# A new hand-written order for the passage from the long convolution into the gated MLP: half-sized copies and turns, another norm path for the first tiles, more filler matmuls

## The chip, the core and the metric

One core of a Trainium2 chip runs the whole program. It has five instruction queues: PE (TensorE: matmuls, with the weight loads shown apart as PEld), DVE (VectorE), ACT (ScalarE), POOL (GpSimd) and SP (SyncE, which issues most DMAs). Each queue runs its own instructions strictly in the order in which the program gave them; queues wait for each other through semaphores. The metric is the device time of one execution in microseconds, lower is better. Before the change it is 304.9 us (median of three runs, 304.87 to 305.95).

## The reference, cut to what matters

Sequence 2048 (16 tiles of 128), width 640 (five units of 128 columns), one batch, bf16.

```python
mod = (silu(c) @ w_mod).reshape(1, 6, 1, -1)            # sa, ca, ga, sb, cb, gb
h = layernorm(x) * (1 + ca) + sa
k_shift = short_conv(A_k, shift_k); kv = k_shift * A_v
y = irfft(rfft(kv, 2S) * rfft(ssm_k, 2S))[:S] + kv * ssm_D
x = x + ga * (h * y)                                     # first half: long convolution, gated
h = layernorm(x) * (1 + cb) + sb
z = gelu(h @ w_in); z1 = z[:, :864]; z2 = layernorm(z[:, 864:])
g = w_sp @ z2 + b_sp
out = x + gb * ((z1 * g) @ w_out)                        # second half: gated MLP mixed along the sequence
```

## The kernel before, in words

The program is a list of 1444 operations, each with a function, a kind and the engines that may run it. A string at the top, `ORDER`, lists all of them once: `P208` means "operation 208, on PE". `Plan.run` walks the string and issues each operation on the engine that its letter names. Nothing else sets the order: on each engine the instructions stand as the string has them, and the framework adds the semaphore waits. Since each operation is numbered by where it is made, inserting one renumbers all that follow.

The first half works unit by unit (u = 0 to 4). Below, `T4_2` is the tile of unit 4, step 2; each unit has eight steps (0 to 7) of two frequency blocks. The kinds that matter, with the lines under which the profile shows them:

- `fwd` (PE, L275, `pu<-X,M`): forward transform of a step into the PSUM tag `pu`, which has two buffers; `pk4_5` is the same for the filter of unit 4, step 5.
- `khc` (ACT, L278, `KH<-pu`): the filter's transform copied out, `KH4_5`.
- `prod` (DVE, L495, `Tf<-pu,KH` or `T<-pu,KH`): the product of a step's `pu` and `KH`. In steps 0, 2, 4, 5, 7 it is written in f32 and two `csum` (L509, `W<-Tf`, POOL or DVE) follow; steps 1, 3, 6 go straight to the inverse.
- `inv` (PE, L275, `pz<-W,G` or `pz<-T,G`): inverse transform into the PSUM tag `pz` (two buffers). `zc` (L278, `Z<-pz`, ACT or DVE): its copy into `Z`.
- `zt` (SP, L777): for units 0 to 3 a DMA turns `Z` into `ZT`; `y` (PE, `sm<-Ebd,ZT`) and `ym` (DVE, L770) make the last transform and multiply it into the gate `gh`.
- `ghm` (L753, POOL or DVE): the modulation of a gate piece, `gh(u, g)`: first times `gca`, then plus `gsa`. `res` (L808): adds a gate piece into the residual `xt`. `ln2` (DVE, L814): statistics of a piece of a row. `modc` (PE): the columns of one modulation vector.

Unit 4 is last, and its `Z` is turned by PE: `zfl` (L831) transposes, `zk` (L278, `X<-pu`, `X<-pz`) copies out, `yl` (PE, `<-Ebd,X`) makes the last transform for four tiles at a time, `yml` (DVE, L856) multiplies, `res` adds, `ln2` and `ag2` (L943) give mean and variance of each row.

The MLP then needs its first tiles. Group 0 (tiles 0 to 3) goes in two pieces of two tiles: `rstd2` (POOL, L218 adds the epsilon, L219 raises to -0.5), `nmr2` (DVE, L947), `zx` (L957 ACT, L959 POOL, L961 DVE: the normalised tile), `hfl` (PE, L972: transposes), `hmod` (L985 DVE, L983 ACT), and then `zz` (PE, L275, `pu<-big,Z` and `pz<-big,Z`: five matmuls of 128x432 each, 16 `zz` to a group of four tiles, four groups) with `gelu` (ACT, L1034). Groups 1 to 3 are turned by a DMA instead (`turn`, L1003, then `hmod2`, L1011). After the last `zz` comes the mixing along the sequence (L1126) and the output projection (L1335, L1348).

`fill` operations are matmuls on the identity, 128x512, whose result is never read (`s<-ident`). They share the PSUM tag `s1`, which has one buffer.

## Time and profile before

| | |
|---|---|
| time of three runs | 304.87, 304.90, 305.95 us |
| span of the profiled execution (first to last instruction) | 303.8 us |
| busy: PE, DVE, POOL, ACT | 293.1, 260.4, 186.8, 164.0 us |
| mean granted TensorE clock | 0.989 |

The profile gives the profiled execution's span alone; a timed run holds 1.1 us beside it (304.9 against 303.8).

A row of the timeline reads: start in us, duration in us, engine, line, operation, output and inputs by tile, shapes, how many instructions were merged (`x2`), and in square brackets how long the engine sat idle before it and which engine released it. Rows of the chain of work read: start, us, engine, tile, line. Rows of the stretches read: from:to, length, busy time of PE, PEld, DVE, ACT, POOL (with the number of instructions), the granted clock of TensorE (1.00 is full), the DMA share and GB/s. Rows of the groups read: line, engine, operation, tiles, shapes, count, busy us, mean ns of one, idle time before. The mapping of a row to an operation of the list is by tile, line and order.

### The profile page before, as it was taken

Reading aid. Unit: us, or ns where it says so; the run is one execution under the profiler, and the core shown is the slowest. Engines: PE = TensorE matmul, PEld = TensorE weight load, DVE = VectorE, ACT = ScalarE, POOL = GpSimd, SP = SyncE. Lnnn points to the kernel's source line nnn. Section 1 sums busy time; section 2 is a strip of 40 time slices with the busy share of each in tenths; the row PEclk is TensorE's granted clock in tenths of the full one; section 3 lists DMA queues with packets and bytes.
Section 4 is the critical chain, followed back from the end, with each engine's and each line's share of the span. In section 5 each row is a group of like instructions: output and inputs, shape, how many; then the busy total and the mean of one; then the engine's idle time right before and its main releaser. Section 6 shows DMA issues by size and latency. Waiting matters only on the chain.

```text
span 303.8 us, 7152 instructions
## 1 busy us (share of the span) xinstructions
PE 293.1 (96%) x2827; PEld 207.0 (68%) x2827; DVE 260.4 (86%) x527; ACT 164.0 (54%) x299; POOL 186.8 (61%) x213
## 2 busy tenths in 40 slices
PE   6899999999999999799999999999999999999996
PEld 2788999999989988645555555555555555665664
DVE  8899999999989999989595988988678798886794
ACT  5989999998888865446665779500111102111110
POOL 5463788839769997577537342099531863476771
PEclk9999999999999999869999999999999999999999
DMA  7999869792397978005997900057654446452433
GB/s 143 270 242 271 194 177 282 134 223 39 77 186 163 287 122 276 2 2 105 157 234 154 197 0 4 0 117 150 132 133 90 102 112 141 102 84 73 91 83 121
DMA packets 117155, 41.57 MB, mean 137 GB/s; under 512 B 102557, under 2 KB 117122, under 8 KB 117122
## 3 DMA queue, kind: packets, MB, share of 16 engines
q1 hardware_dynamic: 116968, 41.08, 62.0%
q8 instruction: 22, 0.36, 0.5%
q14 instruction: 11, 0.09, 0.1%
q10 hardware_dynamic: 154, 0.05, 0.1%
HBM read 16.60 MB, written 2.63 MB: 63 GB/s over the span
## 4 chain that ended last, share of the span: by engine, by line
PE 80%; DVE 8%; SPq 5%; DMA 3%; issue 2%; POOL 1%; ACT 0%; DVEq 0%; POOLq 0%
PE ps L1126 23%; PE pu L275 19%; PE pz L275 17%; PE po L1335 5%; PE sm L275 5%; PE s L275 4%; SPq L570 3%; DVE Tf L495 3%; PE po L1348 3%; DMA ZT<-in_A_v_dram 3%; PE pz L1126 2%; PE pu L1126 1%; DVE Z L616 1%; SPq L585 1%; DVE ot L1394 1%
## 5 line engine op out<-in xcount | busy, mean ns | idle before, releaser
L275 PEld LDWEIGHTS <-Z 128*128 128x128 bf16 x320 | 32.0, 100 | 28.8 <-issue 3.0
L275 PE MATMUL pu<-X,M 128*128 128x128 bf16 (+1 forms) x480 | 45.6, 237 | 0.9 <-DVE Tf L495 0.7
L509 POOL TENSOR_TENSOR W<-Tf 128x256 bf16<-128x256 f32 x42 | 30.7, 745 | 15.0 <-DVE Tf L495 9.0
L275 PEld LDWEIGHTS <-M 128*128 128x128 bf16 x480 | 36.7, 98 | 4.2 <-issue 1.6
L1126 PEld LDWEIGHTS <-S 128*128 128x128 bf16 x256 | 25.0, 98 | 20.8
L275 PE MATMUL pu<-big,Z 128*128 128x432 bf16 x160 | 34.6, 360 | 0.0
L278 ACT CAST X<-s 128x1024 bf16<-128x1024 f32 x32 | 32.7, 1021 | 3.3 <-PE s L275 3.2
L275 PE MATMUL pz<-big,Z 128*128 128x432 bf16 x160 | 33.0, 349 | 0.0
L495 DVE TENSOR_TENSOR Tf<-pu,KH 128x1024 f32<-128x1024 f32 x25 | 30.3, 1215 | 1.2 <-ACT Z L278 0.5
L1132 ACT COPY m<-ps 128x432 f32<-128x432 f32 x7 | 3.6, 521 | 49.8 <-PE ps L1126 41.0
L1126 PEld LDWEIGHTS <-wT 128*128 128x128 bf16 x192 | 18.8, 98 | 15.3
L278 ACT CAST Z<-pz 128x512 bf16<-128x512 f32 x40 | 23.5, 596 | 4.9 <-PE pz L275 4.7
L275 PEld LDWEIGHTS <-G 128*128 128x128 bf16 x330 | 24.6, 98 | 1.8 <-issue 0.4
L278 ACT CAST KH<-pu 128x512 bf16<-128x512 f32 x40 | 23.1, 592 | 3.8 <-PE pu L275 3.4
L1126 PE MATMUL ps<-X,wT 128*128 128x432 bf16 x112 | 22.7, 346 | 0.0
L1126 PE MATMUL ps<-X,S 128*128 128x432 bf16 x112 | 22.6, 346 | 0.0
L1040 DVE BATCH_NORM_STATS2 stz<-X 128x6 f32<-128x432 bf16 x32 | 18.1, 588 | 5.0 <-ACT X L1034 4.9
L1126 PE MATMUL ps<-T,S 128*128 128x432 bf16 x112 | 22.2, 346 | 0.0
L275 PE MATMUL sm<-dg,big 128*128 128x128 bf16 x320 | 20.7, 219 | 1.1 <-DVE Z L616 1.0
L275 PEld LDWEIGHTS <-big 128*128 128x128 bf16 x320 | 18.9, 98 | 2.0 <-issue 1.6
L495 DVE TENSOR_TENSOR T<-pu,KH 128x1024 bf16<-128x1024 f32 x15 | 18.2, 1215 | 1.9 <-PE pu L275 1.8
L275 PEld LDWEIGHTS <-X 128*128 128x128 bf16 x288 | 17.8, 98 | 2.2 <-POOL X L433 0.7
(223 smaller groups left out, 666.7 us busy)
## 6 DMA issues: line engine op xcount, KB each, us to landing
wm<-in_w_mod_dram SPq DMA_DIRECT2D x6, 800.0 KB, 4.9
xt<-in_A_q_dram SPq DMA_DIRECT2D x4, 640.0 KB, 5.6
out_dram<-ot SPq DMA_DIRECT2D x15, 160.0 KB, 1.9
big<-in_B_w_in_dram SPq DMA_DIRECT2D x2, 1080.0 KB, 7.8
X<-in_A_ssm_k_dram SPq DMA_DIRECT2D x4, 512.0 KB, 6.2
ZT<-in_A_v_dram SPq DMA_DIRECT2D x1, 1024.0 KB, 7.6
big<-in_A_v_dram SPq DMA_DIRECT2D x1, 1024.0 KB, 7.8
w_o<-in_B_w_out_dram SPq DMA_DIRECT2D x6, 160.0 KB, 3.5
```

Of the source, the lines that this page charges most:

```text
L275: nc.tensor.matmul(o, lhsT=w, rhs=x, start=start, stop=stop)
L278: (e.copy if e is nc.scalar else e.tensor_copy)(dst, src)
L495: e.tensor_tensor(T_[:], (tl[pu] if src is None else tl[src])[:, :, :, None, :].to_broadcast(shape), tl[KH][:, :, None, :, :].to_broadcast ...
L509: e.tensor_tensor(tl[W][:, :, o, :], T_[:, :, 0, o, :], T_[:, :, 1, 1 - o, :], op=ALU.add if o else ALU.subtract)
L570: e.dma_start_transpose(k_of(u)[:, KPAD + h * m:KPAD + (h + 1) * m], A_k[0, h * m:(h + 1) * m, u * DU:(u + 1) * DU])
L585: e.dma_start(v_of(0, ns.start, NT // n) if u0 == 0 else tl[name][:], v_nat[:, ns, ds])
L616: e.tensor_tensor(dst, tl[ps][:].rearrange("p n (c g) -> p n c g", g=8), v_of(u, i * SCH, SCH).rearrange("p n (c g) -> p n c g", g=8), op= ...
L1040: op("D", "stz", lambda e, i=i, n=n, fc=fc: e.bn_stats(out=stz[:, n, fc, :], in_=tl[z2][:, i, fc * FC:(fc + 1) * FC]), r=[(z2, (i, fc))], ...
L1126: nc.tensor.matmul(ps[:, :FC], lhsT=lhs[:, s_, :], rhs=rhs(s_), start=(s_ == 0 and not more), stop=(s_ == HT - 1), skip_group_check=more)
L1132: e.copy(part[p, m][:], part[p, BANK[m]][:, :FC])
L1335: nc.tensor.matmul(ps[:, :HS], lhsT=w(k), rhs=x(k), start=start and k == 0, stop=stop and k == n - 1, skip_group_check=True)
L1348: e.matmul(po[t, i][:, :hi - lo], lhsT=uTs[t][:fsz[ft], ft, :], rhs=T["w_o"][:fsz[ft], ft, lo:hi], start=(ft == 0), stop=(ft == NFT - 1))
```

## The change

The program has 1462 operations afterwards. `ORDER` is new; up to its 486th entry it runs the same operations on the same engines in the same order, and so do its last 359. What is added or split:

- step 4 of unit 4 (`LAST = 4`, which is the last inverse in either list): its `zc` in two halves of 128x256.
- unit 4's `zfl`: each of four batches of eight transposes in two halves, and each `zk` in two halves of 128x512. In the new list DVE copies both halves of batch 16, the first of batch 8 and the second of batch 24; ACT the other four.
- `yl` of the first four tiles in eight parts instead of four.
- first piece of group 0 (`quick`): the epsilon is added by DVE in the second `ag2`, POOL only raises to -0.5, `nmr2` is gone, and both `zx` run on DVE (before: ACT and POOL).
- `hfl`: by tile instead of by half of the columns.
- unit 4's `res` of groups 1 to 3 may run on POOL (the new list leaves them on DVE).
- six more `fill` of one matmul each; the passage holds `fill8`, `fill7`, `fill4` and the old `fill1` of two matmuls; `fill6` and `fill5` stand far earlier, `fill9` behind the last `zz`.

The two lists decoded, engine by engine, from the product `T3_7` to the passage (number pairs in brackets are unit and group of a gate piece):

```
POOL before: csum W3_5b, ghm(3,3), csum W3_7 x2, ghm(3,0), ghm(4,2), csum W4_0 x2, W4_2 x2, ghm(3,0), csum W4_5 x2,
             W4_7 x2, W4_4a, res(2), ghm(4,1), ghm(4,3), rstd2
POOL after:  csum W3_5b, ghm(3,3), ghm(3,0), ghm(3,0), ghm(4,2), csum W3_7 x2, W4_0 x2, W4_2 x2, W4_5 x2, res(2),
             csum W4_7 x2, W4_4a, res(2), ghm(4,1), res(3), res(3), rstd2
DVE before:  prod T3_7, ym, sbc, ln2 x3, ym, T4_0, ym, T4_3, T4_2, ym, T4_5, T4_1, T4_7, T4_6, T4_4, csum W4_4b, ym, ym,
             ln2, ym, zk, ym, zk, ...
DVE after:   prod T3_7, ghm(4,3), ym, sbc, ln2 x3, ym, ym, ym, zc Z3_7, T4_0, T4_2, T4_5, T4_3, T4_1, T4_7, T4_6, T4_4,
             csum W4_4b, ln2, ym x4, zk x4 (halves), ...
PE before:   inv 3_6, y, fwd pu4_3, inv 3_7, y, pu4_2, modc, pk4_5, pu4_5, pu4_1, inv 4_0, 4_3, pu4_7, inv 4_2, pu4_6,
             inv 4_1, pu4_4, inv 4_5, 4_7, y, 4_6, y, 4_4, y, zfl ...
PE after:    inv 3_6, pu4_2, y, y, modc, inv 3_7, pu4_5, inv 4_0, pk4_5, pu4_3, pu4_1, pu4_7, inv 4_3, 4_2, pu4_6,
             inv 4_1, pu4_4, fill8, inv 4_5, 4_6, y, y, 4_7, 4_4, y, y, zfl halves ...
ACT before:  zc Z3_5, Z3_6, Z3_7, khc KH4_5, gelu table, cbc, zc Z4_0, ...
ACT after:   gelu table, zc Z3_5, Z3_6, cbc, khc KH4_5, zc Z4_0, ...
SP before:   zt ZT3, load w_mod 5, load w_in 0;  after: zt ZT3, load w_in 0, load w_mod 5
```

PE in the passage, after: zfl halves, yl x8, fill7, fill4, yl of tiles 4-7 and 12-15, modc, fill1, vturn, hfl, hfl, yl of tiles 8-11, zz. Before: zfl, modc, yl x4, vturn, yl x3, hfl, hfl, fill1, zz.

The diff, without the string and with its main hunks:

```diff
+LAST = 4
-FILLS = (4, 2, 2, 2, )
+FILLS = (4, 2, 2, 2, 1, 1, 1, 1, 1, 1)
...
-            op("AD", "zc", lambda e: copy(e, tl[Z][:, :, 2 * KP * st:2 * KP * (st + 1), :], tl[pz][:]
+            parts = KP if u == NU - 1 and st == LAST else 1
+            for h in range(parts):
+                k0, k1 = h * KP // parts, (h + 1) * KP // parts
+                op("AD", "zc", lambda e, k0=k0, k1=k1: copy(e, tl[Z][:, :, 2 * (KP * st + k0):2 * (KP * st + k1), :], tl[pz][:, k0:k1]
...
-                tag, k = "pz" if g % 2 else "sm", 4 if g == 0 else 1
+                tag, k = "pz" if g % 2 else "sm", 8 if g == 0 else 1
...
         def norm_piece(g, p, ns, xn2):
+            quick, gs = g == 0 and p == 0, slice(ns[0], ns[-1] + 1)
             for n in ns:
-                op("D", "ag2", lambda e, n=n: e.bn_aggr(out=mv2[:, n, :], in_=st2[:, n, :, :]),
+                def aggregate(e, n=n):
+                    e.bn_aggr(out=mv2[:, n, :], in_=st2[:, n, :, :])
+                    if quick and n == ns[-1]:
+                        e.tensor_scalar(mv2[:, gs, 1], mv2[:, gs, 1], EPS, None, op0=ALU.add)
...
-                op("DAG", "zx", norm, r=[("mv2", n), ("rs2", (g, p)), ("nm2", (g, p))] + [("xt", (u, n)) for u in range(NU)] + ([] if first else [(xn2, "new")]),
+                op("D" if quick else "DAG", "zx", norm, r=[("mv2", n), ("rs2", (g, p))] + ([] if quick else [("nm2", (g, p))]) + [("xt", (u, n)) for u in range(NU)] + ([] if first else [(xn2, "new")]),
```

## The prediction

> **What bounds the kernel now.** I read the page first, then the chain of work in order of time, then stretches for the granted clock, then the timeline of the passage and of the ten microseconds ahead of it.

> ```profile
> span 303.8 us, 7152 instructions
> PE 293.1 (96%) x2827; PEld 207.0 (68%) x2827; DVE 260.4 (86%) x527; ACT 164.0 (54%) x299; POOL 186.8 (61%) x213
> PEclk9999999999999999869999999999999999999999
> ```

> ```profile
> 118.44 0.59 ACT Z L278
> ...
> 129.72 3.60 PE pu L275 x10
> 133.32 2.14 PE pz L275 x10
> ...
> 139.67 1.82 PE pu L275 x10
> ```

> ```profile
> 120.18:123.59 3.41, 3.41 (x112) 3.32 (x109) 3.24 (x9) 2.35 (x4) 0.91 (x1) 1.00 0.22 75
> 123.59:127.00 3.41, 1.98 (x76) 1.88 (x73) 2.96 (x14) 0.92 (x1) 2.13 (x4) 1.00 0.02 5
> 127.00:130.42 3.42, 2.64 (x15) 1.38 (x13) 3.42 (x11) 1.02 (x2) 2.48 (x4) 0.50 0.00 0
> 130.42:133.83 3.41, 3.41 (x11) 1.37 (x9) 3.41 (x13) 1.35 (x2) 3.29 (x4) 0.50 0.00 0
> 134.00:191.00 57.00, 57.00 (x322) 30.82 (x320) 46.13 (x133) 39.83 (x75) 28.02 (x31) 1.00 0.58 114
> ```

> PE bounds the whole; from 134 to 191 it is never idle (57.00 of 57). So a gain in the passage reaches the end only as an earlier, or faster, start of the `zz` stream. The stream starts at 129.72 at half clock (10 matmuls in 3.60 us, later in 1.82) and is at full clock from 133.83. Its first 20 matmuls end at 133.32 + 2.14 = 135.46; at full clock they take 3.64, so the stream stands as if it had begun at 131.8. That is the mark to beat. The half clock costs (133.83 - 129.72)/2 = 2.05 us.

> **Passage, part by part.** From the first transposes (119.08) to the stream:

> ```profile
> 119.08 1.07 PE L831 MATMUL pu<-ident,Z 128*128 128x128 bf16 x16 [0.44 <-ACT Z L278]
> 121.31 1.01 ACT L278 COPY X<-pz 128x1024 bf16<-128x1024 bf16 x1
> 124.43 0.19 POOL L218 TENSOR_SCALAR rstd<-mv 128x2 f32<-128x2 f32 x1 [3.34 <-DVE mv L943]
> 124.70 0.81 POOL L219 TENSOR_TENSOR rstd<-rstd,mhalf 128x2 f32<-128x2 f32 x1
> 125.75 0.92 ACT L957 ACTIVATE Z<-xt,nmr,rstd 128x640 bf16<-128x640 bf16 x1 [2.57 <-DVE nmr L947]
> 125.88 0.87 POOL L959 TENSOR_SCALAR Z<-xt,rstd,nmr 128x640 bf16<-128x640 bf16 x1 [0.36 <-DVE nmr L947]
> 126.81 0.67 PE L972 MATMUL s<-ident,Z 128*128 128x128 bf16 x6 [1.43 <-POOL Z L959]
> 127.58 1.05 DVE L985 TENSOR_SCALAR Z<-s,cb_col,sb_col 128x256 bf16<-128x256 bf16 x3
> 128.00 1.02 ACT L983 ACTIVATE Z<-sm,sb_col,cb_col 128x256 bf16<-128x256 bf16 x2 [1.33 <-PE sm L972]
> 128.69 1.03 PE L275 MATMUL s<-ident 128*128 128x512 bf16 x2 [0.78 <-DVE Z L985]
> L961 DVE TENSOR_SCALAR Z<-xt,mv,rstd 128x640 bf16<-128x640 bf16 x6 | 2.7, 482 | 0.0
> L278 ACT CAST Z<-pz 128x512 bf16<-128x512 f32 x40 | 23.5, 596 | 4.9 <-PE pz L275 4.7
> ```

> - `zc` in halves, both on ACT behind each other: 128x512 takes 0.60 and 128x1024 1.01, so 256 columns take about 0.4, two of them 0.8: a cost of 0.2.
> - `zfl`/`zk` in halves: the last copy ends at 121.31 + 1.01 = 122.32, that is 3.24 after the first transpose. Eight half batches at PE's 0.9 per 16 transposes end at 1.8, seen by ACT at 2.0; ACT's four halves start at about 0.66 and take between 0.5 (half of 1.01) and 0.6 each, the last ending at 2.65. Gain 0.6.
> - Epsilon on DVE: POOL's add costs 124.70 - 124.43 = 0.27, the DVE instruction about 0.1. Gain 0.15.
> - No `nmr2`, both `zx` on DVE: before, pow ends at 125.51 and the later `zx` at 126.75, 1.24 later; two at 0.48 take about 0.9. Gain 0.35. DVE's `ln2`, `yml`, `res` queued behind `ag2` (about 1.0) lie beside POOL's pow.
> - `hfl` by tile: five transposes stand behind the last tile, not ten at half clock: 0.77 (126.81 to 127.58) becomes about 0.5. Gain 0.3.
> - The two-matmul filler moves ahead of `hfl`: before, `hmod` ends at 129.02 and the stream starts at 129.72. Gain 0.7.

> Sum: 2.1 less 0.2, say 2.0 with bounds 1.5 and 2.4. If the clock holds through the passage, 2.05 more. `fill9` stands behind the last `zz` with PE busy: one 128x512 matmul, half of the old pair at full clock, costs 0.2. `fill5` and `fill6` cost the same, up to 0.5 with a wait for their PSUM buffer, but they lie ahead of a point where POOL is late (next part); if that cover goes they cost 0.4 to 1.0. So the passage is worth 2.0 + 2.05 - 0.2 = 3.85.

> **The ten microseconds ahead of it: a new wait.** The new list also rearranges what feeds the last inverse.

> ```profile
> 103.75 1.15 POOL L753 TENSOR_TENSOR gh<-gh,gsa_bf 128x512 bf16<-128x512 bf16 x1
> 104.86 1.41 POOL L509 TENSOR_TENSOR W<-Tf 128x256 bf16<-128x256 f32 x2
> 106.24 2.26 POOL L753 TENSOR_TENSOR gh<-gh,gca_bf 128x512 bf16<-128x512 bf16 x2
> 105.94 1.23 DVE L495 TENSOR_TENSOR Tf<-pu,KH 128x1024 f32<-128x1024 f32 x1
> 107.24 0.60 PE L275 MATMUL pz<-W,G 128*128 128x256 bf16 x6
> 108.98 0.60 PE L275 MATMUL pu<-X,M 128*128 128x256 bf16 x6
> 109.62 0.58 ACT L278 CAST KH<-pu 128x512 bf16<-128x512 f32 x1 [1.16 <-PE pu L275]
> 114.28 1.21 DVE L495 TENSOR_TENSOR T<-pu,KH 128x1024 bf16<-128x1024 f32 x1
> 115.42 1.21 DVE L495 TENSOR_TENSOR Tf<-pu,KH 128x1024 f32<-128x1024 f32 x1
> 116.77 0.98 POOL L509 TENSOR_TENSOR W<-Tf 128x256 bf16<-128x256 f32 x1 [0.85 <-DVE Tf L495]
> 117.80 0.60 PE L275 MATMUL pz<-W,G 128*128 128x256 bf16 x6
> L278 DVE CAST X<-pu 128x512 bf16<-128x512 f32 x3 | 2.0, 681 | 0.0
> ```

> Before, the two sums of `W3_7` run on POOL at 104.86, right behind `ghm(3,3)` (103.75), and three gate multiplies come later. In the new list the three stand ahead of the sums. POOL has no idle time there, so the sums start at 104.86 + 3 x 1.13 = 108.25 and end at 109.6. Step by step:

> 1. `inv 3_7` at 109.65 (before 107.24). Its copy `zc Z3_7` is now on DVE, in front of all products of unit 4: it can start 0.64 later (as `khc` follows `fwd`, 108.98 to 109.62), 110.3, and at 0.68 with overlap lets `T4_0` start at 110.9. Before: 105.94. DVE, which had four `ym` and a `ghm` to do, is idle from about 108.5.
> 2. `T4_0` ends at 112.1, its two sums on POOL at 113.6, `inv 4_0` at 113.65. In PE's queue `pk4_5` is now behind that inverse: 114.1, its copy on ACT from 114.75 to 115.33, and `T4_5` needs it: 115.4. DVE was done with `T4_2` at 113.2: 2.2 us idle.
> 3. Five more products at a pitch of 1.14 (114.28 to 115.42) put `T4_4` at 121.1; the two `pu` buffers and inverses ahead of the `fwd` in PE's queue add 0.5 (next free buffer) to 1.35 (buffers in turn: `pu4_3` waits for `T4_5`). So `T4_4` starts at 121.6 to 122.45 where it started at 115.42: 6.2 to 7.0 late, and its POOL sum, the last inverse (117.80) and the first transposes with it.

> PE meanwhile has little to do. The clock fell at 127.00 and rose at 133.83, 6.83 or 2 x 3.41 apart, so I cut stretches of 3.41 from there and count streamed columns, at 1.82 us for ten times 432 (0.42 ns each).

> ```profile
> 122.82 1.76 PE L275 MATMUL pz<-Ebd,X 128*128 128x16 bf16 x64
> 124.43 0.95 PE L275 MATMUL sm<-Ebd,X 128*128 128x16 bf16 x32
> ```

> The stretch 123.59 to 127.00 holds some 65 of these transforms and four transposes, 1550 columns, 0.65 us: half clock followed. 120.18 to 123.59 holds 16 transposes (2048 columns, 0.86 us) and some 60 transforms, about 1.3 us with the rest: it did not. In the new kernel 109.94 to 113.35 has the end of `inv 3_7` and `pu4_5` (1024 columns), about 0.6 us. By this the clock falls at 113.35, and returns only after a full stretch: 127.00 to 130.42, with PE 2.64 of 3.42 busy, did not bring it back, 130.42 to 133.83 did. From 113.35 each `fwd` takes 0.86 and each direct inverse (2048 columns) 1.72. `T4_5` comes at 116.3. With buffers in turn PE has gaps until 119.8, so full clock returns at 123.59 and `T4_4` ends at 126.6 (116.63 before): 10.0 late. With the next free buffer PE is nearly full from 116.76 on, the clock may return at 120.18, and `T4_4` is 7.7 late. Ends 7.7 and 10.0; no row decides between them, and I take 8.4, a little under the middle, because the low end needs fewer waits.

> [...]

> **Sum.** Delay 8.4 less 3.85: 4.55 slower, against the span 303.8 gives 308.35; with the 1.1 us that a timed run holds beside the span, 309.4 (median of three runs 304.9, to which the same is added). Without the clock's fall it is 6.2 to 7.0 less 3.85: 307.3 to 308.1. With it, 7.7 to 10.0 less 3.85: 308.8 to 311.1.

> Left at nothing: POOL's two `res(3)` ahead of `rstd2` (four operations of 1.15 behind the last sum end about 3.1 after the first transposes, `rstd2` is due at 4.7); `zt` of unit 3 leaves 2.5 us later but its reader `y` does too, and more; `w_in` 0 and `w_mod` 5 change places on SP, both due after 130. The first tiles of group 1:

> ```profile
> 138.88 3.00 SPq L1003 DMA_TRANSPOSE Z<-Z  x1
> 143.97 1.65 POOL L1011 TENSOR_SCALAR Z<-Z,cb_col,sb_col 128x512 bf16<-128x512 bf16 x2 [1.41 <-ACT X L1034]
> ```

> They are ready at about 145.6 and wanted at 131.8 + 16 x 0.91 + 0.6 = 147: 1.4 of slack. In the new list the DMA leaves about 7.7 after the stream starts, lands 5.1 later and needs 2 more: 14.8 against 15.2. I take no stall; at worst 1 us.

> **The rivals.**
> - *The stall without the half clock* (time 307.3 to 308.1, middle 307.7): for it, the stretch's 0.6 us of columns are hardly under the 0.65 that lost the clock, and another cut of the stretches would hold more; against it, PE is idle there for longer than in the stretch that lost it.
> - *The other side: the products run back to back on DVE.* Place: DVE from 103.5 to 117. If POOL's sums and `KH4_5` come before DVE asks for them, the delay is only the work put in front: `ghm(4,3)` at 0.5 and `zc` at 0.6, 1.1, less 3.85: 302.15. It decides below a delay of 2.35 (over 0.5% faster). For it: before, DVE's products stand 1.14 apart there without a wait. Against: POOL's 3 x 1.13 stand in one queue ahead of the sums, without idle time.
> - *Half of it:* `W3_7` comes in time but `KH4_5` does not: `T4_0` at 109.1, `T4_4` 4.3 to 5.1 late, 305.35 to 306.15: no change that can be told.
> - *The passage loses the clock too.* The stretch over the fillers, `hfl` and `yl` has about 1.4 us of columns (four fillers 0.86, ten transposes 0.54), hardly more than the one that kept it. If it falls, up to 2.05 more than the forecast: 311.45. [...]

> **How the numbers follow.** Stall with half clock 0.45, and with the passage's fall as well 0.1; stall alone 0.2; half of it 0.12; back to back 0.13. A measurement of this kernel tells about 0.5% (1.5 us) from no change: 303.4 to 306.4. Faster 0.13, same 0.12, slower 0.75. The range leaves out the back-to-back case and a little at the top: 305.0 to 311.3; the likeliest case's own is 308.8 to 311.1.

> **What would show it.** Right: DVE idle ahead of `zc Z3_7` and again ahead of `T4_5`; POOL with three gate multiplies in a row ahead of the sums of `W3_7`; a granted clock of 0.5 somewhere between 113 and 124; the last inverse 7 to 10 us later than 117.80; and from the first transposes to the stream 8.5 to 9 us instead of 10.64, at clock 1.00. Wrong: `T4_0` starting before 108, or the last inverse within 2 us of its old place; or the passage at half clock as before.

## The result, and the profile after

| | before | after |
|---|---|---|
| time, median of five runs | 305.21 us (304.87 to 305.95) | 314.1 us (313.5 to 315.46) |
| ratio | 1 | 1.0292, 95% interval 1.0265 to 1.0320 |
| span of the profiled execution | 303.8 us | 313.7 us |

The change makes the kernel 8.9 us slower, about twice the 4.5 us of the forecast. The profiled execution of the changed kernel is the slowest of its five runs (315.46), so its span shows a little more than the medians do: 9.9. A timed run holds 1.7 to 1.9 us beside its span wherever both are on record (315.46 against 313.7), not 1.1; the span of 303.8 belongs to a time of about 305.6. The difference that was forecast is not touched by this. A few executions of 389 to 610 us, in some of the experiments, are left out of every median and ratio below.

The mean granted clocks of the five executions are 0.973 (the profiled one), 0.984, 0.984, 0.984 and 0.978. A mean of 0.973 over 313.7 us is 16.9 us at half clock, five stretches of 3.41; a mean of 0.984 is some 10 us, three stretches. So what is said below of where the clock was lost holds for the profiled execution. Where the other four lost it, no trace shows.

The page of the changed kernel, the lines that answer to those of before:

```profile
span 313.7 us, 7168 instructions
PE 299.5 (95%) x2833; PEld 211.3 (67%) x2833; DVE 266.2 (85%) x530; ACT 163.1 (52%) x299; POOL 190.5 (61%) x214
PEclk9999999999999976959999999999999999999999
```

There are now three slices with a lowered clock instead of two, and PE is busy 6.4 us longer (299.5 against 293.1) with six matmuls more: it works more slowly, and hardly more.

To see where the time went I put the two timelines beside each other at products on DVE. Before, the last one ahead of the first difference of the lists and `T3_7`:

```profile
76.36 1.21 DVE L495 TENSOR_TENSOR T<-pu,KH 128x1024 bf16<-128x1024 f32 x1
102.40 1.22 DVE L495 TENSOR_TENSOR Tf<-pu,KH 128x1024 f32<-128x1024 f32 x1
```

After, the same two, then DVE, PE and POOL up to the last product, `T4_4`:

```profile
77.13 1.21 DVE L501 TENSOR_TENSOR T<-pu,KH 128x1024 bf16<-128x1024 f32 x1
104.22 1.20 DVE L501 TENSOR_TENSOR Tf<-pu,KH 128x1024 f32<-128x1024 f32 x1
...
109.47 1.29 DVE L779 TENSOR_TENSOR gh<-gh,sm 128x512 bf16<-128x512 bf16 x2 [1.28 <-PE sm L281]
111.48 0.69 DVE L284 CAST Z<-pz 128x512 bf16<-128x512 f32 x1 [0.72 <-PE pz L281]
112.08 2.35 DVE L501 TENSOR_TENSOR Tf<-pu,KH 128x1024 f32<-128x1024 f32 x2
117.48 1.23 DVE L501 TENSOR_TENSOR Tf<-pu,KH 128x1024 f32<-128x1024 f32 x1 [3.05 <-ACT KH L284]
125.26 1.23 DVE L501 TENSOR_TENSOR Tf<-pu,KH 128x1024 f32<-128x1024 f32 x1 [0.16 <-PE pu L281]
...
110.21 0.76 PE L281 MATMUL sm<-sc_bf,wm 128*128 128x1 bf16 x25 [0.54 <-DVE gh L779]
110.84 0.60 PE L281 MATMUL pz<-W,G 128*128 128x256 bf16 x6
113.35 1.01 PE L281 MATMUL pu<-X,M 128*128 128x256 bf16 x6 [1.91 <-DVE Tf L501]
...
109.25 1.41 POOL L515 TENSOR_TENSOR W<-Tf 128x256 bf16<-128x256 f32 x2
```

And the passage with the first of the stream, and the two waits at the stream's end:

```profile
129.00 1.07 PE L842 MATMUL pu<-ident,Z 128*128 128x128 bf16 x16
131.77 0.61 PE L842 MATMUL pz<-ident,Z 128*128 128x128 bf16 x8 [1.26 <-ACT X L284]
133.35 0.42 DVE L870 TENSOR_TENSOR gh<-gh,sm 128x256 bf16<-128x256 bf16 x1
135.99 0.80 DVE L979 TENSOR_SCALAR Z<-xt,mv,rstd 128x640 bf16<-128x640 bf16 x2
136.40 1.01 PE L281 MATMUL s<-ident 128*128 128x512 bf16 x2
137.54 0.50 PE L993 MATMUL s<-ident,Z 128*128 128x128 bf16 x3
139.49 2.36 PE L281 MATMUL pu<-big,Z 128*128 128x432 bf16 x10
203.02 1.63 PE L1148 MATMUL pz<-X,S 128*128 128x432 bf16 x8 [0.91 <-DVE S L1123]
209.23 1.62 PE L1148 MATMUL pz<-T,wT 128*128 128x432 bf16 x8 [0.19 <-DVE c L1177]
```

Read together (times of before from its rows above and in the prediction, and from this one for its first `zz`):

```profile
129.51 3.81 PE L275 MATMUL pu<-big,Z 128*128 128x432 bf16 x10
```

| point | before | after | later by |
|---|---|---|---|
| last product ahead of the first difference | 76.36 | 77.13 | 0.77 |
| `T3_7` | 102.40 | 104.22 | 1.82 |
| `T4_0` | 105.94 | 112.08 | 6.14 |
| `T4_4` | 115.42 | 125.26 | 9.84 |
| first `zfl` | 119.08 | 129.00 | 9.92 |
| first `zz` | 129.51 | 139.49 | 9.98 |
| end of the span | 303.8 | 313.7 | 9.9 |

0.77 belongs to the two executions (the lists are the same up to there). The rest is lost between 77 and 125 us, and the passage wins nothing back. The stretches of 3.41 us, cut at the changes of the clock (113.0, 123.2, 133.4 and 140.3), show the clock halved twice, in the stall and again in the passage:

```profile
109.55:112.97 3.42, 1.35 (x36) 1.11 (x32) 2.70 (x4) 1.16 (x4) 1.12 (x2) 1.00 0.02 5
112.97:116.38 3.41, 2.49 (x17) 1.94 (x17) 1.46 (x2) 0.00 (x0) 2.77 (x4) 0.50 0.96 184
...
130.03:133.45 3.42, 2.16 (x50) 1.77 (x48) 2.13 (x7) 2.15 (x4) 2.13 (x2) 1.00 0.00 0
133.45:136.86 3.41, 3.35 (x93) 2.62 (x91) 3.27 (x13) 0.17 (x1) 0.71 (x1) 0.50 0.02 5
```

### The profile page after: what moved, and what is told of

It reads as the page before. It is cut to its first block, busy times and chain, and to the rows that moved or that the text cites. A ratio compares the mean times of both kernels' runs of the same rounds, so it can differ in the third digit from the quotient of the medians.

```text
span 313.7 us, 7168 instructions
## 1 busy us (share of the span) xinstructions
PE 299.5 (95%) x2833; PEld 211.3 (67%) x2833; DVE 266.2 (85%) x530; ACT 163.1 (52%) x299; POOL 190.5 (61%) x214
## 4 chain that ended last, share of the span: by engine, by line
PE 31%; DVE 12%; SPq 4%; DMA 3%; POOL 2%; issue 1%; DVEq 0%
PE ps L1148 22%; PE po L1357 5%; PE po L1370 2%; DVE st L823 2%; SPq L1110 2%; DMA Z<-Z 2%; DVE stz L1062 1%; DMA wT<-in_B_w_sp_dram 1%; DVE T L1133 1%; SPq L1220 1%; DVE xt L817 1%; SPq L1025 1%; POOL S L1123 1%; DVE Z L1033 1%; POOL rstd L225 1%
## 5 line engine op out<-in xcount | busy, mean ns | idle before, releaser
L281 PE MATMUL pu<-X,M 128*128 128x128 bf16 (+1 forms) x480 | 48.1, 243 | 3.4 <-DVE Tf L501 2.2
L281 PEld LDWEIGHTS <-Z 128*128 128x128 bf16 x320 | 31.3, 98 | 27.0 <-DVE Z L1007 0.2
L281 PEld LDWEIGHTS <-M 128*128 128x128 bf16 x480 | 38.3, 100 | 8.3 <-issue 5.1
L281 PE MATMUL pu<-big,Z 128*128 128x432 bf16 x160 | 32.8, 349 | 0.0
L281 PEld LDWEIGHTS <-G 128*128 128x128 bf16 x330 | 25.9, 101 | 2.9 <-issue 0.9
L284 ACT CAST Z<-pz 128x512 bf16<-128x512 f32 (+1 forms) x40 | 22.8, 586 | 8.3 <-PE pz L281 7.9
L281 PE MATMUL sm<-dg,big 128*128 128x128 bf16 x320 | 21.9, 226 | 0.1
L281 PEld LDWEIGHTS <-big 128*128 128x128 bf16 x320 | 20.1, 102 | 0.9 <-issue 0.4
```

What stands on the lines that cost most here:

```text
L281: nc.tensor.matmul(o, lhsT=w, rhs=x, start=start, stop=stop)
L284: (e.copy if e is nc.scalar else e.tensor_copy)(dst, src)
```

## The experiments

The theory to begin with: nearly the whole loss arises ahead of the last inverse, through three new waits (POOL's sums of `W3_7`, the copy of `Z3_7` on DVE, the matmuls of `KH4_5`) and the half clock that they bring. The rival: the stretch costs 4 to 5 us and the halves of the passage the rest. "Ratio" is to the kernel before, measured beside it.

**1. The stretch put back.**

```diff
 ORDER of the changed kernel, from the first difference to zc Z4_4:
-  the new order
+  the order of before on all engines (fill5, fill6, fill8 stay behind the same PE operations)
 POOL behind csum W4_4:
-  res(3), res(3), rstd2
+  ghm(4,1), ghm(4,3), res(3), rstd2, res(3), res(2)
```

> The changed kernel, but with the order of before on all engines from the first difference up to the last inverse (the added fillers of that stretch stay), and on POOL up to the first rstd2. Passage and stream as changed. Theory A (the waits ahead of the last inverse are nearly the whole loss): the last inverse stood 9.65 us late, 1.8 of it was there before the stretch, so about 8 less than 314.1: 306.1 with the clock falling in the passage as in the changed kernel, 304 if it holds there. Theory B (the stretch is worth what was forecast for it less the passage's gain, 4 to 5, and the halves cost the rest): 309.5 to 310.

308.5 us, ratio 1.0084 (1.0057 to 1.0111). So 1.0292 - 1.0084, 2.1% or 6.3 us, lies in the stretch: between the two theories (8, and 4 to 5). The trace says more: the first `zfl` stands 119.79 - 103.23 = 16.56 behind `T3_7`, where it stood 16.68 behind it before and 24.78 in the changed kernel, so the whole stall (8.1) is gone. 2.6 us of loss are left. One place of it was my own: POOL's two additions now ran beside the two `zx`, which took 1.24 each where they take 0.40 in the changed kernel (135.99, two in 0.80):

```profile
126.65 2.41 POOL L815 TENSOR_TENSOR xt<-xt,gh 128x512 bf16<-128x512 bf16 x2
126.77 2.47 DVE L977 TENSOR_SCALAR Z<-xt,mv,rstd 128x640 bf16<-128x640 bf16 x2
```

**2. One wait at a time.** Three kernels, each the changed one with one move:

```diff
 e2, POOL:  -ghm(3,0), ghm(3,0), ghm(4,2), csum W3_7, csum W3_7
            +csum W3_7, csum W3_7, ghm(3,0), ghm(3,0), ghm(4,2)
 e3, PE:    -pu4_5, inv 4_0, pk4_5
            +pk4_5, pu4_5, inv 4_0
 e4:        -DVE: zc Z3_7
            +ACT: zc Z3_7 (same place in the string)
```

> The changed kernel with one move: POOL's three gate multiplies go behind the two sums of W3_7. Forecast's step 1 (POOL's queue sets inv 3_7): the sums start 3.4 us sooner and some 3 of it arrive, 311. Theory A (two things end at the same place: PE's own queue, the second transform and the modulation matmuls, ends at 110.84 where the sums end at 110.66): 0 to 0.3 less, 313.8 to 314.1.

> The changed kernel with one move: the matmuls and the copy of KH4_5 go ahead of pu4_5 (in the changed kernel they stand behind inv 4_0). Forecast's step 2: T4_5 starts at about 115.3 instead of 117.48, so 2.1 less, 312, more if the half clock shortens by a stretch of 3.41 (310.3). Rival: the two pu buffers hold pu4_5 until T4_2 is done and nothing is gained, 314.

> The changed kernel with one move: the copy of Z3_7 goes from DVE to ACT, so that no product waits for inv 3_7. Theory A: DVE's ym still wait for PE's transforms, T4_0 starts at 110.76 instead of 112.08, 1.3 less and, with KH4_5 earlier by the same, 312 to 312.8. Forecast's steps 1 and 2 (the copy is what holds the products): T4_0 at 108 to 109, 3 to 4 less and the clock kept, 308 to 311.

Ratios: e2 1.0298 (1.0257 to 1.0339), e3 1.0206 (1.0171 to 1.0241), e4 1.0217 (1.0165 to 1.0270). Taking POOL's multiplies out of the way of the sums gives nothing. In e2's timeline the sums are done at 106.7, and the inverse still runs at 110.35, behind the modulation matmuls, and `T4_0` at 111.60:

```profile
105.14 1.59 POOL L513 TENSOR_TENSOR W<-Tf 128x256 bf16<-128x256 f32 x2
...
109.73 0.76 PE L279 MATMUL sm<-sc_bf,wm 128*128 128x1 bf16 x25 [0.55 <-DVE gh L777]
110.35 0.60 PE L279 MATMUL pz<-W,G 128*128 128x256 bf16 x6
```

The other two each end in a gain of some 2.5 us. In e3 `T4_5` starts at 115.28, that is 11.63 behind `T3_7` instead of 13.26: 1.6 sooner, a little less than the 2.1 expected, and the half clock lasts one stretch (3.41 us) instead of three. In e4 `T4_0` comes 1.4 sooner (6.45 behind `T3_7` instead of 7.86), and the half clock lasts two stretches. What the copy then uncovers is the three `ym`, which in the new list stand ahead of `T4_0` and themselves wait for PE's transforms.

**3. The passage, mended step by step on the base of e1.**

```diff
 e5, POOL:  -ghm(4,1), ghm(4,3), res(3), rstd2, res(3), res(2)
            +ghm(4,1), ghm(4,3), res(3), res(3), res(2), rstd2
 e6, PE:    -zfl 16a, 0a, 16b, 0b, 24a, 8a, 24b, 8b      (a, b: the halves of a batch; copies between them)
            +zfl 0a, 0b, 16a, 16b, 24a, 24b, 8a, 8b, each pair followed by its copies, a on DVE, b on ACT
 e7, PE:    +fill5, fill6, fill8 behind the first yl, fill9 behind modc; yl of tiles 12 to 15 behind hfl
 e8:        +the order of before from the first zz on
```

> The kernel with the stretch put back (308.5), and POOL's two residual additions, which there ran beside the two zx on DVE, put ahead of the first rstd2. There the two zx took 2.47 us together, in the changed kernel 0.80. Theory (an addition on POOL slows a DVE instruction that reads and writes SBUF at the same time): the two zx take about 0.8 again, hfl and the stream come 1.3 to 1.6 sooner, 307.0. Rival (the zx were slow for another reason, or the stream waits elsewhere): 308.5.

> As the run before it in this call (POOL's additions ahead), and the last transposes listed PSUM tile by PSUM tile: both halves of a tile, then its two copies, one on DVE and one on ACT; the transforms in that order too. In the changed kernel the second eight of the pz pair waited 1.26 us for ACT's copy of the first half of the same PSUM tile, and the pu pair was copied only when all sixteen were done. Theory (the wait is kept per PSUM tile, not per half): no such wait, the last copy ends about 1.3 sooner, 305.7. Rival (the chain is held by the copies' own time on ACT and DVE): 306.7 to 307.

> As e6_turns_by_tile, and the four added single fillers that stood elsewhere (ahead in the stretch, and behind the stream) moved into the passage, one transform of the last group behind hfl. Counted over the runs so far, full clock was kept where PE streamed 1.31 us or more of columns in a stretch of 3.41 and lost at 1.18 or less; here every stretch of the passage has at least 1.35. Theory: no half clock in the passage, about 2 to 2.5 less for 0.2 to 0.4 of fillers on the path, 303.5. Rival (the fillers only lengthen PE's queue, the clock falls anyhow): 306 to 306.5.

> As e7_fillers_in, with the order of before from the first zz to the end. In the changed kernel the mixing waits 0.91 us for a sum on DVE and 0.19 for another. Theory: both waits go, 1.1 less than e7_fillers_in, 302.4. Rival (DVE or ACT is the bound of the stream's end either way): no change against e7_fillers_in.

| run | median | ratio | runs compared |
|---|---|---|---|
| e5 | 307.17 | 1.0047 (1.0021 to 1.0073) | 305.10 to 307.97 |
| e6 | 306.85 | 1.0046 (1.0028 to 1.0063) | 305.98 to 307.59 |
| e7 | 307.15 | 1.0041 (1.0001 to 1.0080) | 304.70, 304.80, 304.84, 304.96, and six from 306.89 to 308.97 |
| e8 | 308.26 | 1.0089 (1.0055 to 1.0124) | 308.22 to 308.48 |

e5 shows the collision of POOL and DVE: the two `zx` take 0.80 again, and the median falls by 1.3 (1.1 by the ratios, whose intervals overlap a little). Three of its eight executions also kept the clock throughout, which none of e1's did, so a part of the fall can be the clock's. In its profiled execution the clock is 1.00 to the end, and the passage takes 129.16 - 119.89 = 9.27 us:

```profile
127.21 0.80 DVE L977 TENSOR_SCALAR Z<-xt,mv,rstd 128x640 bf16<-128x640 bf16 x2
```

In e6 PE's wait of 1.26 between the halves is gone and the first `yml` comes 3.86 after the first `zfl` (120.01), not 4.35; but POOL's addition then meets DVE's residual, 1.11 instead of 0.29:

```profile
120.91 1.06 PE L840 MATMUL pz<-ident,Z 128*128 128x128 bf16 x16
...
123.87 0.42 DVE L868 TENSOR_TENSOR gh<-gh,sm 128x256 bf16<-128x256 bf16 x1
124.32 1.11 DVE L815 TENSOR_TENSOR xt<-xt,gh 128x256 bf16<-128x256 bf16 x1
```

Even so 3.86 is no less than the 3.73 of the whole copies before (119.08 to 122.81). The halves don't run beside each other: in e7 ACT waits for DVE's copy of the other half of the same PSUM tile, although its transposes are done (the eight of that tile end at 119.59; DVE's first copy ends at 120.33, and ACT's starts at 120.42).

```profile
119.91 0.75 DVE L282 COPY X<-pu 128x512 bf16<-128x512 bf16 x2
120.42 1.07 ACT L282 COPY X<-pu 128x512 bf16<-128x512 bf16 x2 [1.50 <-DVE X L282]
```

So the wait stood for the PSUM tile, not for a half of it: 0.83 here (119.59 to 120.42), and 1.26 on PE's side in the changed kernel, where the second eight transposes stood behind a copy out of the same tile. Why it is kept for the whole tile no run shows.

e7 has two sorts of executions: four at 304.7 to 305.0 with the clock at 1.00 throughout, six at 306.9 to 309.0 with a mean of 0.983 to 0.989. The likely reason is that its fillers hold the clock only for some places of the 3.41 us cut (last section). e8 lost the clock in each of the three executions compared (0.982 to 0.983), so its comparison with e7 doesn't show what the stream's order is worth.

**4. The order of the stream alone**, put back in the changed kernel:

```diff
 from the first zz to the end:  -the new order   +the order of before
```

> The changed kernel with the order of before from the first zz to the end, and nothing else. Theory (the new order of the stream costs 0.91 us at the wait for a sum on DVE and 0.19 at another): 1.1 to 1.5 less than the changed kernel, a ratio of 1.024 to 1.026 to the kernel before. Rival (the stream's order is as good, its end is late only because its start is): 1.029.

316.67 us, ratio 1.0345 (1.032 to 1.037): slower than the changed kernel, though the two intervals just meet. Its 0.91 and 0.19 are gone, but PE now waits at the second `zz` pair and at the second `hfl`:

```profile
141.98 1.07 PE L279 MATMUL pz<-big,Z 128*128 128x432 bf16 x5 [1.16 <-DVE gh L868]
...
144.47 0.34 PE L991 MATMUL s<-ident,Z 128*128 128x128 bf16 x3 [1.41 <-POOL Z L975]
```

Its clock also falls once more, from 144.83 to 148.25. Both theories of that expectation fall: the old order of the stream doesn't suit the new passage.

**5. The clock in the stall.** The changed kernel with nine more single fillers:

```diff
 PE:  inv 3_7, +fill x4, pu4_5, inv 4_0, pk4_5, +fill x2, pu4_3, +fill x3, pu4_1
```

> The changed kernel with nine single fillers in the stretch where PE waits: four behind inv 3_7, two behind the matmuls of KH4_5, three behind pu4_3. The waits stay as they are, only the clock is to be held. Forecast's step 2 (the half clock lengthens the stall by 2 to 3): KH4_5 is copied at 116.0 instead of 116.8, the products then follow each other at 1.17, T4_4 starts at 122.5 to 123.5 instead of 125.26, 311.5 to 312.3. Rival (DVE and the waits set the stretch, not PE's speed): 314.

313.44 us, ratio 1.0271 (1.0218 to 1.0324); the runs go from 312.88 to 315.57. The profiled execution (312.88) shows no lowered clock in the stall or behind it (its first ten `zz` take 2.02 us, half clock took 3.6 before), and `T4_4` starts at 122.58 as expected. Counted from the last common product (76.86 here, 77.13 in the changed kernel) that is 45.72 against 48.13: the half clock made 2.4 of the stall, the order of the waits the rest. With the 1.4 of a passage at full clock (9.09 against 10.49 from the first `zfl` to the first `zz`) that is 3.8, of which 2.3 reach the end (from the same product, 311.1 - 76.86 = 234.24 against 313.7 - 77.13 = 236.57). The other 1.5 is given back in the stream, where PE waits twice for POOL, 1.2 in all (0.94 at 166.65).

The other executions have means of 0.983 to 0.995, so they lost the clock somewhere, and the median moves by 0.7 only.

**6. The kernel before with fillers, then with the short norm path.** The experiments suggested that the clock of the passage is worth some 2 us and that little else of the change is worth anything. So:

```diff
 e9, the kernel before:
-FILLS = (4, 2, 2, 2, )
+FILLS = (4, 2, 2, 2, 1, 1, 1, 1, 1, 1, 1, )
 PE:  zfl, zfl, y, zfl, zfl, +fill x2, yl (tiles 0-3), +fill x3, yl (12-15), +fill x2, modc, fill1, vturn, yl (4-7),
      hfl, hfl, yl (8-11), zz
 e10: e9, and of the change norm_piece and hfl by tile; yl (4-7) behind hfl; POOL's res(2) behind the second rstd2
 e13: e10, DVE: +ln2(3,2), ag2, ag2, yml, nmr2 right behind the first three hmod; POOL: zx ahead of its res
 e14: e13, DVE: +the second three hmod ahead of ghm(4,2), res(3), and statistics of tiles 4 to 7
```

> The kernel before, with nothing of the change but seven single 128x512 fillers in its passage: two behind the last transposes, three behind the first transforms, two behind the next, the old pair ahead of hfl, one group of transforms behind it. Every 3.41 us of the passage then streams at least 1.35 us of columns. Theory (the half clock of the passage costs the kernel before 2.05 us, and a stretch with 1.31 us or more of columns keeps the clock): the stream starts at about 129.1 at full clock where it stood as if begun at 131.8, 2.3 to 2.7 less than before: 302.6 to 303. Rival (the fillers lengthen PE's queue and the clock falls at some other cut): 305 to 306.

> As e9_before_fillers, and of the change the short way of the first two tiles alone: epsilon on DVE, no nmr2, both zx on DVE, hfl by tile; POOL has one residual addition ahead of rstd2 and the other behind the second rstd2, so that none runs beside the zx. Whole copies, the order of before elsewhere. Theory: hfl starts 1.0 to 1.4 sooner than in the kernel before, and the stream with it, 301.3 to 302. Rival (PE's queue of fillers and transforms is then what ends last): as e9_before_fillers.

> As e10_fillers_quick, where PE waited 3.37 us for the second two tiles because DVE reached nmr2 only at 135.99, with DVE's order mended: the statistics of tiles 2 and 3 and their nmr2 right behind the first hmod, POOL's zx of tile 2 right behind its rstd2, its residual additions after that. Theory (the earlier stream only uncovered that wait): the wait goes but for 0.3, 2.5 to 3.5 less than e10_fillers_quick and 1 to 1.5 less than e9_before_fillers, ratio 0.990. Rival (the statistics cannot come sooner since PE's transforms come late): 0.995 to 1.0.

> As e13_fillers_quick2, where PE waited 2.70 and 0.42 us for the hmod of tiles 2 and 3 (138.49 on DVE, their transposes done at 133.4), with those three hmod put ahead of a gate multiply, a residual addition and the statistics of tiles 4 to 7 on DVE. Theory (only the place in DVE's order is wrong): both waits go, ratio 0.990 to 0.994. Rival (DVE is full from the passage to the third group, so what is put ahead makes the next thing late): the wait comes back at the first tiles of the next group, 1.000 or more.

| run | median | ratio |
|---|---|---|
| e9 | 304.23 | 0.9951 (0.9933 to 0.9968) |
| e10 | 308.94 | 1.0099 (1.0065 to 1.0132) |
| e13 | 308.22 | 1.0094 (1.0063 to 1.0124) |
| e14 | 310.13 | 1.0145 (1.0106 to 1.0184) |

e9 is faster than both kernels: 1.5 us less than before, 0.5%, with an interval that doesn't reach 1. All four of its runs have the clock at 1.00 (0.999 in one), and they lie within 303.44 to 304.39. It fell short of its 2.3 to 2.7: the stream does start at full clock, at 128.78, but PE then waits 0.55 for the second two tiles. e9 also puts the old pair of fillers ahead of `hfl` and one group of `yl` behind it; what these two moves are worth without the fillers was not run.

```profile
128.78 1.99 PE L275 MATMUL pu<-big,Z 128*128 128x432 bf16 x10
133.13 0.51 PE L972 MATMUL s<-ident,Z 128*128 128x128 bf16 x6 [0.55 <-POOL Z L959]
```

The short norm path on top of it, with the moves listed beside it, costs more than it gives, three times, and each mend moves the wait on: in e10 to the second `hfl`, in e13 to the second `hmod`, in e14 to the `gelu` that stands on ACT behind a `zx` of group 1. One line each, from e10, e13 and e14:

```profile
137.32 0.48 PE L981 MATMUL s<-ident,Z 128*128 128x128 bf16 x3 [3.37 <-POOL Z L965]
```

```profile
138.88 0.54 PE L277 MATMUL pz<-big,Z 128*128 128x432 bf16 x1 [2.70 <-DVE Z L995]
```

```profile
143.12 1.96 PE L277 MATMUL pu<-big,Z 128*128 128x432 bf16 x5 [4.93 <-ACT X L1044]
```

The outcome is that of the rival of e14's expectation: the wait comes back further on. Its reason, that DVE is full, is not shown. The `zx` on ACT waits for DVE's `nmr2`, and DVE is itself idle ahead of that, for POOL's `rstd2`:

```profile
141.06 0.16 DVE L953 SCALAR_TENSOR_TENSOR nmr<-mv,rstd 128x4 f32<-128x4 f32 x1 [1.15 <-POOL rstd L221]
```

Whether some other order could hold the two `zx` (0.80) that the path puts on DVE isn't shown; three orders couldn't.

## Why the prediction was right and wrong

The step that failed is the gain that was set against the stall: the passage was to give 4.05 us and gave 1.7, and two more terms, the early fillers and the stream, stood at nothing or nearly. The stall itself came in at its size. By the prediction's own terms, for the profiled executions: the mark of the stream is where it would have begun at full clock. After, 20 matmuls from 139.49 end at 141.68 + 1.99 = 143.67, less 3.64 is 140.03, that is 11.03 after the first `zfl`; before it was 131.8 - 119.08 = 12.72.

| term | forecast | measured | from |
|---|---|---|---|
| stall, `T3_7` to the first `zfl` | +8.4 | +8.1 | 9.92 - 1.82 |
| `fill5` and `fill6` | 0 | +1.05 | 1.82 - 0.77 |
| passage, first `zfl` to the mark | -4.05 | -1.7 | 11.03 - 12.72 |
| stream to the end | +0.2 | +1.7 | 9.9 less the other rows |
| the executions themselves | - | +0.77 | the first row |
| sum | +4.55 | +9.9 | |

- **The stall's size was right, one of its reasons wrong.** 8.1 for 8.4. Steps 2 and 3 hold: `T4_5` waits 3.05 for `KH4_5`, and the clock falls at 113.0 (forecast 113.35) and returns at 123.2 (123.59). e3 shows the first, e12 the second and the clock's share: 2.4. That the instants agree to 0.4 is luck: the forecast took its cut from the trace of before, and in the traces of e2, e3, e4 and e11 the clock falls there anywhere from 111.91 to 114.11. The size is in part luck too. With full clock the way from `T3_7` to `T4_4` is 122.58 - 103.95 = 18.63 in e12, against 13.02 before: a stall of 5.6 and 2.4 for the clock, where the forecast's 8.4 holds 6.2 to 7.0 and 1.4 to 2.2: two errors that partly cancel. Step 1 fails: POOL's three multiplies ahead of the sums do stand there in a row, but e2 shows that they cost nothing. PE's own queue (two `y`, then `modc`) ends at 110.84, just after the sums at 110.66. The forecast had DVE idle from 108.5 for want of the copy; it is the `ym` ahead of the copy that wait for PE (109.47, 1.28 idle). Two queues that end together hid each other, so naming the wrong one cost the forecast nothing.
- **`fill5` and `fill6` at nothing: wrong.** The cover that the text named (POOL's lateness) lies behind `T3_7`, and there they have already cost 1.05. The text's price without that cover, 0.4 to 1.0, was about right. In all nine traces with the two in place (the changed kernel, e1 to e6, e11, e12) `T3_7` stands 27.09 to 27.12 behind the last common product, in all seven without them 26.03 to 26.05. e7, which moves them away, has `T3_7` at 102.23 - 76.18 = 26.05 behind that product, as before (26.04), where the changed kernel has 27.09:

```profile
76.18 1.21 DVE L499 TENSOR_TENSOR T<-pu,KH 128x1024 bf16<-128x1024 f32 x1
...
102.23 1.23 DVE L499 TENSOR_TENSOR Tf<-pu,KH 128x1024 f32<-128x1024 f32 x1
```

- **The passage: the term that was mis-sized most.** Its rival with chance 0.1, the clock falling there too, came in, and with it the prediction's own sign of being wrong, the passage at half clock as before. The forecast rested on 1.4 us of columns in the stretch over the fillers; the cut lay elsewhere, and 130.03 to 133.45 streamed 1.15. It was no bad luck either: by the count in the last section, an estimate, some three of four cuts through this order of the passage lose the clock (laid through e12's trace, where it ran at full clock). That cost about 1.6: 10.49 against the 9.27 of e5 up to the stream, and 0.4 in it ((140.27 - 139.49)/2). The halves, taken as a gain of 0.6, cost 0.6: the first `yml` comes 133.35 - 129.00 = 4.35 after the first `zfl`, not 3.1 and not the 3.73 of before, because the second eight transposes wait 1.26 for a copy out of the same PSUM tile. The filler moved ahead, taken as a gain of 0.7, stood at half clock in front of `hfl`: the `zx` are done at 136.79, `hfl` starts at 137.54. Epsilon, `nmr2` and `zx` were right: pow's end to the second `zx`'s end is 0.9 as forecast (135.89 to 136.79); the epsilon itself took 0.17 on DVE (134.93) where the forecast estimated 0.1.
- **The stream: left out.** The forecast took a later or earlier start of the `zz` as the whole effect. 0.91 and 0.19 at 203.02 and 209.23 and `fill9`'s 0.2 are 1.3 of the 1.7; the rest stays open. The two waits belong to the new order of the stream: every trace with it (the changed kernel, e1 to e7, e12) has them, 0.9 to 1.1 and 0.2, and none with the old one (before, e8, e11) does. Which of DVE's moves makes them isn't shown.
- **The other rivals.** Stall without half clock: no. Products back to back, and half the delay: no. No change without effect: no.

The direction was right with a chance of 0.75. The range ended at 311.3, 2.8 below the median: hardly above the stall's own upper end (311.1), with nothing for a passage that loses the clock as well (311.45 with the middle of the stall), for the fillers or for the stream.

## What to carry to other kernels

Before a wait is charged to one queue, look at every queue that ends at the same instruction: here two ended within 0.2 us, mending one gave nothing, and the second had to be read from its own rows. A gain ahead of a saturated engine is only worth what the next engine can follow: ask of each instruction that now comes earlier whether its inputs do (in e10 PE waited 3.37 us for one that didn't). And where an engine's clock falls when it streams little, as PE's did here after 3,056 columns or fewer in 3.41 us, idle slots of its queue can be filled on purpose (e9, with clock 1.00 and 1.5 us less than before), with enough in each stretch that the result doesn't hang on where the stretches are cut.

## What the runs showed of the hardware

```profile
125.56:128.98 3.42, 2.14 (x39) 1.92 (x36) 2.06 (x6) 1.64 (x4) 3.22 (x3) 1.00 0.00 0
128.98:132.39 3.41, 3.36 (x112) 2.87 (x110) 3.30 (x12) 0.58 (x1) 0.53 (x1) 1.00 0.00 0
132.39:135.80 3.41, 3.41 (x64) 2.46 (x61) 2.39 (x9) 0.98 (x4) 0.19 (x1) 0.50 0.02 5
```

```profile
125.69 1.07 PE L840 MATMUL pu<-ident,Z 128*128 128x128 bf16 x16
126.59 0.61 PE L840 MATMUL pz<-ident,Z 128*128 128x128 bf16 x8
128.46 0.61 PE L840 MATMUL pz<-ident,Z 128*128 128x128 bf16 x8 [1.26 <-ACT X L282]
128.90 1.10 PE L279 MATMUL sm<-Ebd,X 128*128 128x16 bf16 x32
129.86 0.81 PE L279 MATMUL s<-ident 128*128 128x512 bf16 x2
130.51 1.75 PE L279 MATMUL pz<-Ebd,X 128*128 128x16 bf16 x64
```

The first holds 32 transposes of 128 columns, 4,096; the second 32 and some 60 transforms of 16 columns and two fillers of 512, about 2,520. So the transposes (matmuls on the identity in the profile) count: the first stretch has hardly anything else and kept the clock. The cut is not tied to the start of the program: the first change stands at 7.54 us in the kernel before and at 10.57 in the changed one (pairs of 128x256 follow each other at 0.43 ahead of it, at 0.22 behind it), though the lists begin alike. That would explain why one kernel (e7) gives 304.8 or 308. As an estimate from the traces, I laid the 3.41 us cut at every place through three passages that ran at full clock: a stretch with fewer than 3,100 columns comes up for 46% of the places in e7 (six of its ten executions lost the clock), for 17% in e9 (none of four) and for 74% in e12, whose passage has the changed kernel's order.

**POOL and DVE in each other's way.** A 128x640 `zx` on DVE took 0.40 alone (changed kernel, 135.99) and 1.24 beside POOL's additions (e1, 126.77), a 128x256 residual 0.29 (changed kernel, 133.81) and 1.11 (e6, 124.32). With the additions ahead of `rstd2` the `zx` took 0.40 again (e5). What the two engines share there no run shows. A copy out of PSUM on DVE was not slowed: in the changed kernel one of 128x512 took 0.42 beside POOL's additions (130.55) and 0.42 without them (132.26).
